# A fused attention and two mixture-of-experts kernel: one kind of matmul at a time, soft experts in pairs, a spread shared slot, a split last slot

## The chip, the cores and the metric

The kernel runs on one core of a Trainium2 chip, as one program. The metric is the device time of one execution in microseconds (us); less is better. Engines are named as the profile names them: PE is the matrix engine (PEld its weight loads), DVE, ACT and POOL are the vector, scalar and GpSimd engines, and SP is the engine whose queue issues most of the DMAs.

## The reference

Three layers follow one another on 1536 tokens of 512 features (2 batches of 768 tokens, 8 heads of 64). Everything is fp32.

```python
# 1 attention: key kept if among the first 8 (global) or 0..95 behind the query
scores = q @ k.T / 8 - slope[head] * dist        # -1e9 where not kept
a = softmax(scores, -1);  x = (a @ v) laid out as [1536, 512]
# 2 soft mixture: 8 experts, 4 slots each
logits = x @ phi                                 # [1536, 32]
d = softmax(logits, 0);   slot_in = d.T @ x      # over all tokens
h = relu(slot_in[e] @ w1[e]);  slot_out[e] = h @ w2[e]
x = softmax(logits, 1) @ slot_out
# 3 second mixture: 8 other experts, the best 2 for each token
noisy = x @ w_gate + log1p(exp(x @ w_noise)) * noise
out[token] += weight * (relu(x[token] @ w1[e]) @ w2[e])   # for its 2 experts
```

Each expert has w1 of 512x1024 and w2 of 1024x512, so each mixture reads 32 MB of weights.

## The kernel before, in words

**Attention** (functions `scores` to `stX`, loop over T = 0..12) takes 12 tiles of 128 queries, each in two halves, b0 = 2T and b1 = 2T + 1. For a half, PE multiplies 16 pairs of 64x64 weights by 167 keys into two PSUM banks (line 201); DVE adds the position bias and takes the row maximum in one custom instruction per bank half, four of them, into a tile `Tt` (205); ACT takes four exponentials with their sums (212); DVE inverts the sums (218, 219); POOL multiplies them in and lays the result out by key in `Pb` (227, 229); PE turns it, eight 128x128 transposes per half (237, tile `pt`); ACT copies that to `PT` (241). PE multiplies `PT` by the values `vt` (260), DVE copies the result, `xT` (267), and PE turns this back to tokens (`stX`, 277). POOL also copies the 8 global rows of the values from a small tile `gv` into each new `vt` (269, 271). After tiles 3, 7, 10 and 11 a segment (`seg`) updates the token softmax of layer 2 and adds into `U`. The order of the instructions on each engine is the order of this code.

**Weights.** The 32 MB of layer 2 come as 32 units of 1 MB, each half of a w1 or of a w2. Sixteen are issued during attention (line 372, in two DMAs of 0.5 MB, paced by `PACE`). Sixteen follow on the SP queue behind attention (682, two halves per unit): eight into a pool that lies where attention's tiles were, and eight into tiles that the first sixteen held (`AGAIN`). Then come the weights of layer 3 by `load_part` (735). SP runs its queue in order, and each issue waits for the eighth before it to have landed. Six DMAs of 0.5 MB that set the output to zero (`zero`, from a tile `zt`) are issued in tiles 5 to 10.

**Soft experts** (`ffn_a` 720, `ffn_t` 753, `ffn_b` 766): per expert PE does 32 matmuls with 32 weight columns for the first product, two 128x128 transposes of its activations, and 16 matmuls for the second product, which sums over all experts in one bank. The loop does a of expert e, t of e - 1, b of e - 2.

**Second mixture.** Weights become fp16 pairs (high and low part). Each expert has three slots of 128 tokens (24 in all, `NOWN`), each with 8 first products (1205), and three times 8 second products (1293), whose sum ACT scales into `ys` (1305) and POOL adds to the output with an indirect DMA (1311). A further "shared" slot (`Shared`) takes the tokens left over, 32 rows for each of four experts side by side: 8 steps `mm` (1176) of 12 small matmuls, a scaling, a joining matmul and one indirect add (1192). The table `SHARE` says after which part of which slot each of its steps stands: "0", "a", "m" and "p" are points inside a slot. The last slot's sum is scaled half on DVE (1302), then half on ACT (1303).

Adds of different experts may meet the same output row, so such an add waits for the one before to land; the three adds of one expert don't wait for one another.

Of the kernel before, what the change touches and what calls it, by code (L numbers as in the profile page):

```python
# [23 lines left out]
AGAIN = [0, 1, 4, 5, 8, 9, 12, 13]  # L24
PACE = lambda i: 1 + 4 * i // 3
KLOADS = {1: 3, 4: 6, 6: 9}
VLOADS = {1: 2, 4: 4, 6: 6, 8: 8, 10: 10}
ZEROS = [5, 6, 7, 8, 9, 10]
# [13 lines left out]
         (21, "0", "mm", 6), (21, "0", "mm", 7), (21, "0", "end"), (21, "a", "join"), (21, "m", "add", NOWN)]  # L42
# [6 lines left out]
NXS = 5  # L49
# [13 lines left out]
def emit(tc, d, near=True, stop=None):  # L63
    nc = tc.nc
    es = ExitStack()
    with es:
# [53 lines left out]
        phis = ac.tile([128, 4, 32], F32, name="phis")  # L120
        if near:
            ac.tile([128, 128], F32, name="Lsb")
            ac.tile([128, 128], F32, name="Et")
# [9 lines left out]
        pw = ps_o.tile([128, 512], F32, name="o")  # L133
# [57 lines left out]
        def scores(i, nm):  # L191
            Tt = wk.tile([128, 4, 167], F32, name="Tt", bufs=2)
            st = [ps_s.tile([128, 2, 167], F32, name="s") for _ in range(2)]
            m = i // 2 % 6
            for n in (2 * i, 2 * i + 1):
                T, p = divmod(n, 4)
                for t in range(2):
                    a = KS * m + 64 * t
                    for h in range(2):
                        g, r = slice(64 * h, 64 * h + 64), 64 * (h ^ t)  # L200
                        nc.tensor.matmul(st[t][r:r + 64, n % 2, :], qd[T % NQ][g, p, 64 * t:64 * t + 64], kx[g, p, a:a + 167],  # L201
                                         start=True, stop=True, tile_position=(64 * h, r))
            for k in range(4):
                j, t = divmod(k, 2)
                nc.vector.tensor_tensor_reduce(Tt[:, k], st[t][:, j], bias[:, int(m == 0), 2 * (i % 2) + j, t], -0.125, 1e30, ALU.add,  # L205
                                               ALU.min, nm[:, k:k + 1])
            S[i] = Tt
# [7 lines left out]
        def norm(i, st):  # L215
            Pu = S[i]
            r = sm.tile([128, 4], F32, name="r", bufs=3)
            nc.vector.tensor_scalar(r, st, 1e-9, None, ALU.add)
            nc.vector.reciprocal(r, r)  # L219
            Pn = Pb[i % NP]  # L220
# [52 lines left out]
        def stX(T):  # L273
            j = T % 4
            pxx = (ps_o if T < NT - 1 else ps_t).tile([128, 4, 128], F32, name="o" if T < NT - 1 else "pt")
# [22 lines left out]
        def seg(t0, w, psl):  # L298
# [10 lines left out]
            Lsb = ac.tile([128, 128], F32, name="Lsb", bufs=1)  # L309
            Et = ac.tile([128, 128], F32, name="Et", bufs=1)  # L310
# [7 lines left out]
            if near:  # L318
                nc.vector.tensor_copy(Lsb[P], psl[P])
                yield  # L320
                pe = (ps_o if late else ps_l).tile([128, 2, 128], F32, name="o" if late else "psl")
# [13 lines left out]
            else:  # L335
                pe = ps_o.tile([128, 2, 128], F32, name="o")
# [6 lines left out]
            pu = (ps_s if near and late else ps_o).tile([128, 512], F32, name="s" if near and late else "o")  # L343
# [13 lines left out]
        zt = lo.tile([128, 512], F32, name="zt")  # L357
        nc.gpsimd.memset(zt, 0.0)

        def zero(a, b):  # L360
            nc.sync.dma_start(out=out[a:b].rearrange("(p t) c -> p t c", p=128),
                              in_=zt.unsqueeze(1).to_broadcast([128, (b - a) // 128, 512]))

        def all_units():
            for k in range(NWA + NW):
                todo.extend(load_unit(k, wst if k < NW else wa, f"w{k}", 2))
            todo.reverse()
# [15 lines left out]
        def attention_near():  # L383
# [17 lines left out]
            segs, held = {}, {}  # L401

            def head(T):
                more_w(PACE(2 * T))
                st, nm = [sm.tile([128, 4], F32, name=k, bufs=3) for k in ("st", "nm")]
                scores(2 * T, nm)
                exps(2 * T, st, nm, (0, 1))
                return st, nm

            st0, nm = head(0)  # L410
            for T in range(NT + 1):
                new, b0, b1 = T < NT, 2 * T, 2 * T + 1
                if T in KLOADS:
                    load_k(KLOADS[T], 3)
                if T + 3 < NT:
                    load_q(T + 3)
                if T in VLOADS:
                    load_v(VLOADS[T])
                if T in ZEROS:
                    zero(256 * ZEROS.index(T), 256 * ZEROS.index(T) + 256)  # L420
                old = segs.pop(T - 3, None)
                if T - 4 in held:
                    list(held.pop(T - 4))
                if T < 2:
                    tables(1 - T, 2, 4)
                outs = [turn(n, True) for n in (2 * b0 - 4, 2 * b0 - 3)] if T else []
                for k, o in enumerate(outs):
                    o()
                    if new:
                        exps(b0, st0, nm, (2 + k,))  # L430
                if not new:
                    stX(T - 2)
                    segs[T - 2] = seg(*SEGS[T - 2], logits(*SEGS[T - 2]))
                if new and not outs:
                    exps(b0, st0, nm, (2, 3))
                if new:
                    more_w(PACE(b1))
                    st, nm = [sm.tile([128, 4], F32, name=k, bufs=3) for k in ("st", "nm")]
                    scores(b1, nm)
                    norm(b0, st0)  # L440
                    exps(b1, st, nm, (0,))
                outs = [turn(n, True) for n in (2 * b1 - 4, 2 * b1 - 3)] if T else []
                for k, o in enumerate(outs):
                    o()
                    if new:
                        exps(b1, st, nm, (1 + k,))
                if new:
                    exps(b1, st, nm, (3,) if outs else (1, 2, 3))
                if T == 0:
                    tables(0, 0, 2)  # L450
                fill(FILL.get(T, 0))
                if old:
                    next(old)
                if new and 0 <= T - 2:
                    stX(T - 2)
                if old:
                    next(old)
                if new and T - 2 in SEGS:
                    segs[T - 2] = seg(*SEGS[T - 2], logits(*SEGS[T - 2]))
                if T - 2 in SEGS:  # L460
                    next(segs[T - 2])
                if T + 1 < NT:
                    st0, nm = head(T + 1)
                if new:
                    norm(b1, st)
                if T - 2 in SEGS:
                    next(segs[T - 2])
                if T:
                    for n in range(2 * b0 - 4, 2 * b0):
                        values(n)  # L470
                if old:
                    next(old)
                    held[T - 3] = old
                if T:
                    valued(T - 1)
                if T == 1:
                    nc.gpsimd.memset(rn[0], 1e30)
                    nc.gpsimd.memset(rs, 0.0)
                    nc.gpsimd.memset(U, 0.0)
            more_w(2 * (NWA + NW))  # L480
            old = segs[T - 2]
# [10 lines left out]
        def attention_any():  # L492
# [4 lines left out]
            zero(0, NTOK)  # L497
# [81 lines left out]
        Lsb = ac.tile([128, 128], F32, name="Lsb", bufs=1)  # L579
        Et = ac.tile([128, 128], F32, name="Et", bufs=1)  # L580
# [25 lines left out]
        psi = ps_o.tile([128, 4, 32], F32, name="o")  # L606
# [134 lines left out]
        def ffn_a(e):  # L741
# [3 lines left out]
            hs = mw.tile([128, 256], F32, name="hs")  # L745
# [3 lines left out]
        def ffn_t(e):  # L749
            hs = hTs[e]  # L750
            pt = pm_([128, 2, 128])
            for i in range(2):
                nc.tensor.transpose(pt[:, i], hs[:, 128 * i:128 * i + 128], ident)

            hT = mw.tile([128, 2, 4, 32], F32, name="hT", bufs=3)
            nc.gpsimd.memset(hT, 0.0)
            es_ = slice(4 * e, 4 * e + 4)
            nc.vector.tensor_copy(hT[:, :, :, es_], pt.rearrange("p a (g s) -> p a g s", g=4)[:, :, :, es_])
            hTs[e] = hT
# [9 lines left out]
        with tc.manual_schedule(engines=hands):  # L769
            for e in range(NE + 2):  # L770
                if e < NE:
                    ffn_a(e)
                if 0 <= e - 1 < NE:
# [987 lines left out]
```

## Time and profile before

| what | value |
|---|---|
| median of 3 runs | 324.84 us (323.02 to 325.19) |
| the execution that was profiled, its own time | 324.2 us |
| its span, first to last instruction | 322.4 us |
| PE busy | 300.5 us, 93% |
| ACT, DVE, POOL busy | 206.9, 197.6, 129.5 us |
| data moved | 89.25 MB, mean 277 GB/s |
| PE clock granted | 0.98 over the span, below full in one early slice (16 to 24 us) and after the last matmul |

The profile is of one execution. Its stages, read from which lines run when: attention up to about 92 us, the joining of layer 2's slots up to 99, soft experts from 99 to 131, routing of the second mixture up to about 165 (slots begin inside it), slots up to 314, and the last add's landing up to 322. The time outside the span is 324.2 - 322.4 = 1.8 us.

### The profile page before, as it was taken

The numbers are of one execution on the slowest core, as the hardware profiler recorded it, in microseconds if no ns is written. First come the engines' busy times: TensorE is split into PE (matmuls) and PEld (weight loads), VectorE is DVE, ScalarE is ACT, GpSimd is POOL, SyncE is SP. The second block draws the span as 40 slices with busy tenths as digits, with TensorE's granted clock in tenths as the row PEclk, the third lists the DMA queues.
The fourth block names the chain that finished last, engine by engine and source line by source line (L and its number), as shares of the span: only waits on it lengthen the run. The fifth ranks groups of instructions, "written<-read, shape, count | busy, mean of one in ns | idle before, by whom it ended". The sixth has DMA issues, their size and how long they took to land. (4 is left out here: it accounts for less than half of the span.)

```text
span 322.4 us, 7769 instructions
## 1 busy us (share of the span) xinstructions
PE 300.5 (93%) x2860; PEld 169.7 (53%) x2860; DVE 197.6 (61%) x724; ACT 206.9 (64%) x490; POOL 129.5 (40%) x165
## 2 busy tenths in 40 slices
PE   8599999899999999998988999999999999999990
PEld 3367877678766443444544445554454445544540
DVE  1746667667555000299768796969687586996210
ACT  2759887888633111299759786869788686685400
POOL 3355555464601100213443857642617335261131
PEclk9959999999999999999999999999999999999996
DMA  8999999997999999999899779497999943404352
GB/s 252 362 401 347 331 370 403 405 405 250 406 409 410 408 408 403 411 407 409 325 344 344 167 176 245 64 349 241 222 334 337 339 73 43 68 1 53 48 67 39
DMA packets 30651, 89.25 MB, mean 277 GB/s; under 512 B 2816, under 2 KB 6656, under 8 KB 30608
## 3 DMA queue, kind: packets, MB, share of 16 engines
q1 hardware_dynamic: 25920, 80.70, 65.7%
q0 software_dynamic: 4400, 7.48, 15.7%
q10 hardware_dynamic: 288, 0.52, 0.6%
q8 instruction: 24, 0.39, 0.5%
q14 instruction: 19, 0.16, 0.1%
HBM read 78.55 MB, written 10.14 MB: 275 GB/s over the span
## 5 line engine op out<-in xcount | busy, mean ns | idle before, releaser
L1293 PE MATMUL y<-w2hl,hh 128*128 128x512 f16 x552 | 125.1, 379 | 0.8 <-ACT w2hl L1307 0.8
L1293 PEld LDWEIGHTS <-hh 128*128 128x128 f16 x552 | 52.2, 98 | 61.7 <-issue 4.8
L227 POOL TENSOR_TENSOR Pb<-Tt,r 128x668 f32<-128x668 f32 x24 | 32.1, 1336 | 43.9 <-DVE r L219 32.2
L212 ACT ACTIVATE Tt<-Tt,nm 128x167 f32<-128x167 f32 x96 | 40.8, 427 | 10.3 <-DVE nm L205 10.2
L1214 DVE SCALAR_TENSOR_TENSOR hh<-h,hh 128x512 f16<-128x512 f32 x46 | 29.6, 684 | 20.7 <-ACT hh L1206 20.7
L1311 POOL DMA_INDIRECT out_y<-ys,sidx x15 | 27.9, 1857 | 30.4 <-ACT ys L1305 16.1
L205 DVE CUSTOM_DVE_ANT_0 Tt<-s,bias 128x167 f32<-128x167 f32 x96 | 26.1, 328 | 22.6 <-POOL Pb L229 9.3
L890 DVE SCALAR_TENSOR_TENSOR w2hl<-w,pm,w2hl 128x1024 f16<-128x1024 f32 x28 | 35.2, 1280 | 3.3 <-ACT w2hl L887 2.4
L1329 POOL DMA_INDIRECT cT<-ctab,gidx x25 | 27.6, 1105 | 13.7 <-DVE pm L844 6.7
L1206 ACT ACTIVATE hh<-h 128x512 f16<-128x512 f32 x46 | 25.1, 598 | 12.0 <-PE h L1205 10.1
L241 ACT ACTIVATE PT<-pt 128x512 f32<-128x512 f32 (+1 forms) x48 | 26.2, 551 | 8.4 <-PE pt L237 8.2
L887 ACT ACTIVATE w2hl<-w,pm 128x1024 f16<-128x1024 f32 x28 | 31.2, 1147 | 0.2 <-DVE pm L843 0.2
L237 PE MATMUL pt<-c,Pb 128*128 128x128 f32 x176 | 25.5, 287 | 5.1 <-POOL Pb L227 2.6
L858 ACT ACTIVATE w2hl<-w 128x1024 f16<-128x1024 f32 x28 | 29.5, 1059 | 0.0
L237 PEld LDWEIGHTS pt<-c,Pb 128*128 128x128 f32 x176 | 19.3, 144 | 12.4 <-POOL Pb L229 4.4
L1311 POOL DMA_INDIRECT out_y<-c,sidx x7 | 11.2, 1595 | 33.1 <-ACT w2hl L887 12.6
L260 PE MATMUL px<-PT,vt 128*64 128x128 f32 x352 | 22.7, 283 | 0.0
L201 PE MATMUL s<-kx,qd 64*64 64x167 f32 x384 | 21.0, 321 | 1.6 <-DVE nm L205 1.5
L260 PEld LDWEIGHTS px<-PT,vt 128*64 128x64 f32 x352 | 19.7, 141 | 2.9 <-issue 2.5
L212 ACT ACTIVATION_READ_ACCUMULATOR Tt<-Tt,nm 128x1 f32 x96 | 18.3, 191 | 0.0
L201 PEld LDWEIGHTS s<-kx,qd 64*64 64x64 f32 x384 | 13.2, 135 | 7.4 <-issue 6.4
L1205 PEld LDWEIGHTS <-Gst 128*128 128x128 f16 x192 | 12.7, 98 | 7.1 <-issue 1.8
(315 smaller groups left out, 445.6 us busy)
## 6 DMA issues: line engine op xcount, KB each, us to landing
w<-in_w2b SPq DMA_DIRECT2D x14, 1024.0 KB, 12.7
x<-in_w1b SPq DMA_DIRECT2D x12, 1024.0 KB, 10.2
w<-in_w1a SPq DMA_DIRECT2D x16, 512.0 KB, 8.8
w<-in_w2a SPq DMA_DIRECT2D x16, 512.0 KB, 10.2
w<-in_w1a SPq DMA_DIRECT2D x8, 1024.0 KB, 14.6
w<-in_w2a SPq DMA_DIRECT2D x8, 1024.0 KB, 11.7
vt<-in_va SPq DMA_DIRECT2D x6, 512.0 KB, 5.8
out_y<-zt SPq DMA_DIRECT2D x6, 512.0 KB, 7.1
```

The source lines that it names most:

```text
L201: nc.tensor.matmul(st[t][r:r + 64, n % 2, :], qd[T % NQ][g, p, 64 * t:64 * t + 64], kx[g, p, a:a + 167], start=True, stop=True, tile_posit ...
L212: nc.scalar.activation(Tt[:, k], Tt[:, k], AF.Exp, bias=nm[:, k:k + 1], scale=-1.0, accum_out=st[:, k:k + 1])
L227: nc.gpsimd.tensor_tensor(wide(Pn, 33, 264 + 64, 528, 167), Pu.rearrange("p (a t) c -> p a t c", t=2), rb(167), ALU.mult)
L237: nc.tensor.transpose(pt[:, ch, t], Pn[:, 2 * (n % 2) + t, 136 * ch:136 * ch + 128], ident)
L260: nc.tensor.matmul(px[64 * h:64 * h + 64, p, :], vv[:, c:c + 64], cols_, start=(ch == 0 or m == 0), stop=(ch == 1))
L858: nc.scalar.activation(w2hl[:, self.r, 1, 2 * q:2 * q + 2], self.quarter(q), AF.Abs, accum_out=self.wm[:, q:q + 1])
L887: nc.scalar.activation(w2hl[:, self.r, 0, 2 * q:2 * q + 2], self.quarter(q), AF.Copy, scale=self.sw)
L890: nc.vector.scalar_tensor_tensor(w2hl[:, self.r, 1, 2 * q:2 * q + 2], self.quarter(q), self.sw, w2hl[:, self.r, 0, 2 * q:2 * q + 2], ALU.m ...
L1214: nc.vector.scalar_tensor_tensor(hh[:, 1, 4 * q:4 * q + 4], phs[q], 0.0, hh[:, 0, 4 * q:4 * q + 4], ALU.max, ALU.subtract)
L1293: nc.tensor.matmul(py, hh[:, hx, f], w2hl[:, e, wx, f], start=(n == 0), stop=(n == 23))
L1311: o = nc.gpsimd.indirect_dma_start(out=out, out_offset=bass.IndirectOffsetOnAxis(ap=sidx[:, j:j + 1], axis=0), in_=ys, in_offset=None, com ...
L1329: nc.gpsimd.indirect_dma_start(out=cgf[:, place(n)], out_offset=None, in_=ctab, in_offset=bass.IndirectOffsetOnAxis(ap=gidx[:, n:n + 1], a ...
```

## The change

- Attention does one kind of PE work per tile: all 32 score matmuls of a tile in a row into four banks, then the 32 value matmuls of tile T - 2 (T - 1 before), then the turns of tile T - 1 with `stX` of T - 3 between them. `Tt` has three buffers instead of two. The normalisation of b1 stands in the next tile's iteration.
- Pool `ps_s` grows to four banks, `ps_x` shrinks to one, `ps_o` is gone.
- The output's zeros become one DMA behind the first slots' start (after `go`), before the loads of expert 3.
- The units come in another order (`UNITS`): w1 of experts 0 to 5 and w2 of 0 and 1 during attention, then w1 of 6, 7 and w2 of 2, 3, then w2 of 4 to 7 into tiles of the w1 of experts 2 to 5.
- The soft experts run in pairs: two a, one t with four transposes for both, two b.
- The shared slot's `mm` steps stand in slots 20, 21 and 22 (20 and 21 before), its add between those of slots 21 and 22 (between 20 and 21 before).
- The last slot's second product is done for 256 columns and then for the other 256, in two banks, with 48 matmuls of half the width; ACT scales both halves.

```diff
-AGAIN = [0, 1, 4, 5, 8, 9, 12, 13]
+UNITS = [4 * e + i for e in range(6) for i in (0, 1)] + [2, 3, 6, 7]
+UNITS += [24, 25, 28, 29, 10, 11, 14, 15, 18, 19, 22, 23, 26, 27, 30, 31]
+AGAIN = [4, 5, 6, 7, 8, 9, 10, 11]
-VLOADS = {1: 2, 4: 4, 6: 6, 8: 8, 10: 10}
-ZEROS = [5, 6, 7, 8, 9, 10]
+VLOADS = {0: 2, 4: 4, 6: 6, 8: 8, 10: 10}
...
-         (20, "a", "mm", 1), (20, "a", "copy", 3), (20, "a", "copy", 4), (20, "m", "mm", 2), (20, "m", "mm", 3),
-         (20, "m", "copy", 5), (20, "p", "copy", 6), (20, "b", "mm", 4), (20, "b", "mm", 5), (21, "0", "copy", 7),
-         (21, "0", "mm", 6), (21, "0", "mm", 7), (21, "0", "end"), (21, "a", "join"), (21, "m", "add", NOWN)]
+         (20, "m", "copy", 3), (20, "p", "copy", 4), (21, "0", "mm", 2), (21, "0", "mm", 3), (21, "0", "copy", 5),
+         (21, "a", "copy", 6), (21, "m", "mm", 4), (21, "m", "mm", 5), (21, "m", "copy", 7), (22, "0", "mm", 6), (22, "0", "mm", 7),
+         (22, "0", "end"), (22, "m", "join"), (22, "p", "add", NOWN)]
...
-        ps_s = pool("ps_s", 2, s_ps, space=PSUM)
+        ps_s = pool("ps_s", 4, s_ps, space=PSUM)
-        ps_x = pool("ps_x", 2, s_ps, space=PSUM)
+        ps_x = pool("ps_x", 1, s_ps, space=PSUM)
-        ps_o = pool("ps_o", 1, s_ps, space=PSUM)
-            wk.tile([128, 4, 167], F32, name="Tt", bufs=2)
+            wk.tile([128, 4, 167], F32, name="Tt", bufs=3)
...
             for T in range(NT + 1):
                 new, b0, b1 = T < NT, 2 * T, 2 * T + 1
+                last = sums.pop(T - 1, None)
+                if new:
+                    bank = scores(T)
+                    maxima(b0, bank, nm0, (0, 1))
+                if last:
+                    r1 = inverse(last)
+                    norm(b0 - 1, r1)
+                if new:
+                    maxima(b0, bank, nm0, (2, 3))
+                    exps(b0, st0, nm0)
+                    maxima(b1, bank, nm1, range(4))
+                    exps(b1, st1, nm1, (0,))
...
+                if T >= 2:
+                    for n in range(4 * T - 8, 4 * T - 4):
+                        values(n)
+                    valued(T - 2)
+                    if T in VLOADS:
+                        load_v(VLOADS[T])
+                outs = [turn(4 * T - 4 + p, True) for p in (0, 1)] if T else []
+                for o in outs:
+                    o()
+                if new:
+                    norm(b0, r0)
+                    exps(b1, st1, nm1, (1,))
+                if T >= 3:
+                    stX(T - 3)
+                if T:
+                    turn(4 * T - 2)
...
+                if T:
+                    turn(4 * T - 1)
+                if new:
+                    exps(b1, st1, nm1, (2, 3))
...
-            for o, src in load_unit(k, wb if i < NWB else wst if t < NW else wa, f"w{t}"):
+            for o, src in load_unit(UNITS[k], wb if i < NWB else wst if t < NW else wa, f"w{t}"):
...
+            ffn(ffn_a, 0)
+            halves()
+            ffn(ffn_a, 1)
+            ffn_t(0)
+            ffn(ffn_a, 2)
+            ffn_t(1)
+            ffn(ffn_b, 0)
+            make_ct()
+            ffn(ffn_a, 3)
+            ffn_t(2)
+            ffn(ffn_b, 1)
+            ffn_t(3)
+            ffn(ffn_b, 2)
+            ffn(ffn_b, 3)
...
+            if j == NOWN - 1:
+                for c in (slice(0, 256), slice(256, 512)):
+                    py = py if c.start == 0 else ps_y.tile([128, 512], F32, name="y")
+                    for i, (hx, wx) in enumerate(((0, 0), (0, 1), (1, 0))):
+                        for f in range(8):
+                            nc.tensor.matmul(py[:, c], hh[:, hx, f], w2hl[:, e, wx, f, c], start=(i == 0 and f == 0),
+                                             stop=(i == 2 and f == 7))
...
+                    nc.scalar.activation(ys[:, c], py[:, c], AF.Copy, scale=gs)
...
         nc.sync.value_load(go, min_val=1, max_val=1)
+        zero(0, NTOK)
         for i in range(2):
             fetch(3, i)
```

PE, one tile in the middle of attention, before (`s` scores, `px` values, `pt` turns, `o` the turn back to tokens):

```order
L201 MATMUL s<-kx,qd_106 64x167 x8
L260 MATMUL px<-PT,vt 64x128 x16
L237 MATMUL pt<-c_71,Pb_111 128x128 x8
L201 MATMUL s<-kx,qd_106 64x167 x8
L237 MATMUL pt<-c_71,Pb_112 128x128 x8
L277 MATMUL o<-c_71,xT 128x128 x4
```

and the same tile now:

```order
L199 MATMUL s<-kx,qd_103 64x167 x16
L266 MATMUL px<-PT,vt 64x128 x16
L243 MATMUL pt<-c_71,Pb_108 128x128 x8
L283 MATMUL s<-c_71,xT 128x128 x4
L243 MATMUL pt<-c_71,Pb_109 128x128 x8
```

Two runs of scores have become one, and the turn back to tokens stands between the two runs of turns.

SP, the last weight loads of attention and the first of the second half, before, with the engines whose semaphores each waits for:

```order
L372 DMA w_179<-in_w2a 128x1024 [waits DMAHW1_49]
L372 DMA w_179<-in_w2a 128x1024 [waits DMAHW2_49]
L682 DMA w_1712<-in_w1a 128x2x1024 [waits DMAHW3_49,PE_49]
L682 DMA w_1714<-in_w1a 128x2x1024 [waits DMAHW4_49,DVE_49]
L682 DMA w_1716<-in_w2a 128x2x1024 [waits DMAHW5_49,DVE_49,Activation_49]
```

and now:

```order
L371 DMA w_174<-in_w2a 128x1024 [waits DMAHW3_49]
L371 DMA w_174<-in_w2a 128x1024 [waits DMAHW4_49]
L675 DMA w_1700<-in_w1a 128x2x1024 [waits DMAHW5_49,Pool_49]
L675 DMA w_1702<-in_w1a 128x2x1024 [waits DMAHW6_49,DVE_49,PE_49]
L675 DMA w_1704<-in_w1a 128x2x1024 [waits DMAHW7_49]
```

The first load of the second half waited for PE (the last half-tile's scores); now it waits for POOL, for the last copy out of `gv`, whose place in SBUF it takes.

POOL, the last four adds to the output before:

```order
L1192 DMA out_y<-x_3943,sidx 1920x512 [waits DMASW5_49,DMASW4_49,DMASW6_49,DMASW3_49,Activation_49]
L1311 DMA out_y<-c_4237,sidx 1920x512 [waits DMASW6_49,Activation_49]
...
L1311 DMA out_y<-ys,sidx 1920x512 [waits DMASW0_49,Activation_49]
...
L1311 DMA out_y<-ys,sidx 1920x512 [waits Activation_49]
```

and now:

```order
L1328 DMA out_y<-c_4190,sidx 1920x512 [waits DMASW5_49,DMASW4_49,DMASW6_49,DMASW3_49,Activation_49]
L1333 MEMSET go 1x1 [waits Pool_49]
L1198 DMA out_y<-x_3943,sidx 1920x512 [waits DMASW6_49,Activation_49]
L1328 DMA out_y<-ys,sidx 1920x512 [waits DMASW7_49,DMASW0_49,Activation_49]
L1333 MEMSET go 1x1 [waits Pool_49]
L1328 DMA out_y<-ys,sidx 1920x512 [waits Activation_49]
```

The shared slot's add (line 1192 before, 1198 now) stands one add later, and the add of slot 22 now waits for its landing.

## Rows read from the trace of the kernel before

**Rows 1.** The page's rate of all transfers, in 40 slices of 8.06 us.

```profile
GB/s 252 362 401 347 331 370 403 405 405 250 406 409 410 408 408 403 411 407 409 325 344 344 167 176 245 64 349 241 222 334 337 339 73 43 68 1 53 48 67 39
```

**Rows 2.** Timeline of PE's weight loads, one tile (start, duration, idle before, releaser).

```profile
31.92 0.49 PEld L201 LDWEIGHTS s<-kx,qd 64*64 64x64 f32 x16 [0.17 <-issue]
32.65 1.73 PEld L260 LDWEIGHTS px<-PT,vt 128*64 128x64 f32 x32 [0.24 <-issue]
34.55 0.85 PEld L237 LDWEIGHTS pt<-c,Pb 128*128 128x128 f32 x8 [0.17 <-issue]
...
36.65 0.86 PEld L237 LDWEIGHTS pt<-c,Pb 128*128 128x128 f32 x8 [0.59 <-POOL Pb L229]
37.48 0.47 PEld L277 LDWEIGHTS o<-c,xT 128*128 128x128 f32 x4
```

**Rows 3.** Timeline of DVE, the longer of its two waits in that tile.

```profile
36.63 0.33 DVE L205 CUSTOM_DVE_ANT_0 Tt<-s,bias 128x167 f32<-128x167 f32 x1 [1.13 <-POOL Pb L229]
```

**Rows 4.** Timeline of ACT in that tile, one instruction of each kind.

```profile
32.21 0.58 ACT L241 ACTIVATE PT<-pt 128x512 f32<-128x512 f32 x1
...
33.10 0.42 ACT L212 ACTIVATE Tt<-Tt,nm 128x167 f32<-128x167 f32 x1
```

**Rows 5.** Timeline of POOL: the normalisation of b0 in tiles 3 and 11, then b1 of tile 11.

```profile
32.01 1.30 POOL L227 TENSOR_TENSOR Pb<-Tt,r 128x668 f32<-128x668 f32 x1 [1.05 <-ACT PT L241]
...
84.71 1.30 POOL L227 TENSOR_TENSOR Pb<-Tt,r 128x668 f32<-128x668 f32 x1 [1.97 <-ACT PT L241]
...
87.00 1.30 POOL L227 TENSOR_TENSOR Pb<-Tt,r 128x668 f32<-128x668 f32 x1 [0.79 <-DVE r L219]
...
88.44 0.60 POOL L271 COPY vt<-gv 8x512 f32<-8x512 f32 x1
```

**Rows 6.** Timeline of the SP queue, first load of the second half.

```profile
83.09 0.91 SPq L682 DMA_DIRECT2D w<-in_w1a  x2
```

**Rows 7.** Tile `w`, the DMA issued at 105.2 us (fourteenth load of that half).

```profile
L682 SPq DMA_DIRECT2D w<-in_w1a x1: 1067/1067/1067, 105.2 to 105.2; - x1
...
DMA to landing us min/median/max: 17.8/17.8/17.8
```

**Rows 8.** Tile `w`, the 0.5 MB DMA issued at 34.9 us: its landing.

```profile
DMA to landing us min/median/max: 4.4/4.4/4.4
```

**Rows 9.** Timeline of PE's weight loads, one soft expert, and the stage's last load.

```profile
121.53 0.20 PEld L753 LDWEIGHTS m<-c,hs 128*128 128x128 f32 x2 [0.41 <-issue]
121.89 0.16 PEld L766 LDWEIGHTS y<-w,hT 128*32 128x32 f32 x8 [0.17 <-issue]
...
125.47 0.20 PEld L753 LDWEIGHTS m<-c,hs 128*128 128x128 f32 x2 [0.41 <-issue]
...
130.67 0.13 PEld L766 LDWEIGHTS y<-w,hT 128*32 128x32 f32 x4 [0.30 <-issue]
```

**Rows 10.** Tile `w2hl`, first half of expert 2's w1, issued at 137.7: its landing.

```profile
DMA to landing us min/median/max: 14.4/14.4/14.4
```

**Rows 11.** Timeline of PE's weight loads, the first products with w1 of experts 2 and 3.

```profile
154.40 1.45 PEld L720 LDWEIGHTS pg<-w2hl,soT 128*32 128x32 f32 x32
...
188.35 1.45 PEld L720 LDWEIGHTS pg<-x,soT 128*32 128x32 f32 x32
```

**Rows 12.** Timeline of ACT, a slot beside that routing.

```profile
157.57 0.60 ACT L1206 ACTIVATE hh<-h 128x512 f16<-128x512 f32 x1 [1.50 <-PE h L1205]
```

**Rows 13.** Timeline of POOL, the first add and three of the last.

```profile
180.14 1.63 POOL L1311 DMA_INDIRECT out_y<-w2hl,sidx  x1 [0.30 <-issue]
...
300.61 1.57 POOL L1192 DMA_INDIRECT out_y<-x,sidx  x1 [4.23 <-ACT x L1189]
...
306.32 1.56 POOL L1311 DMA_INDIRECT out_y<-c,sidx  x1 [4.14 <-ACT hh L1206]
...
315.39 1.57 POOL L1311 DMA_INDIRECT out_y<-ys,sidx  x1 [4.00 <-ACTq L1554]
```

**Rows 14.** Timeline of ACT, its half of the last slot's scaling.

```profile
314.51 0.47 ACT L1303 ACTIVATE ys<-y,gsc 128x256 f32<-128x256 f32 x1 [5.01 <-DVE ys L1302]
```

More of the change, by code (lines that the diff above doesn't have):

```diff
@@ L219, in norm @@
             nc.vector.reciprocal(r, r)
+            return r
+        def norm(i, r):
+            Pu = S.pop(i)
             Pn = Pb[i % NP]
@@ L274, in stX @@
             j = T % 4
[L275 removed]
+            pxx = (ps_s if T < NT - 1 else ps_t).tile([128, 4, 128], F32, name="s" if T < NT - 1 else "pt")
             for p in range(4):
@@ L320, in seg @@
                 yield
-                pe = (ps_o if late else ps_l).tile([128, 2, 128], F32, name="o" if late else "psl")
+                pe = (ps_s if late else ps_l).tile([128, 2, 128], F32, name="s" if late else "psl")
                 nc.tensor.transpose(pe[:, 0, P], Et[P], ident[P, P])
@@ L342, in seg @@
                 nc.vector.tensor_copy(Ek[:, P], pe[:, 0, P])
-            pu = (ps_s if near and late else ps_o).tile([128, 512], F32, name="s" if near and late else "o")
+            pu = (ps_l if near and not late else ps_s).tile([128, 512], F32, name="psl" if near and not late else "s")
             for j in range(w):
@@ L355, in emit @@
         todo = []
[L357 to L362, printed above, removed]
         def all_units():
             for k in range(NWA + NW):
-                todo.extend(load_unit(k, wst if k < NW else wa, f"w{k}", 2))
+                todo.extend(load_unit(UNITS[k], wst if k < NW else wa, f"w{k}", 2))
             todo.reverse()
@@ L400, in attention_near @@
             tables(1, 1, 2)
[L401 to L410, printed above, removed]
+            segs, sums = {}, {}
             for T in range(NT + 1):
                 new, b0, b1 = T < NT, 2 * T, 2 * T + 1
+                more_w(PACE(b0))
                 if T in KLOADS:
@@ L431, in attention_near @@
[L431 to L435, printed above, removed]
-                if new:
[L437 to L446, printed above, removed]
-                if new:
-                    exps(b1, st, nm, (3,) if outs else (1, 2, 3))
+                last = sums.pop(T - 1, None)
+                if new:
+                    (st0, nm0), (st1, nm1) = [[sm.tile([128, 4], F32, name=k, bufs=3) for k in ("st", "nm")] for _ in range(2)]
+                    bank = scores(T)
+                    maxima(b0, bank, nm0, (0, 1))
@@ new lines, in attention_near @@
+                if last:
[4 more added lines that the diff above has]
+                    exps(b0, st0, nm0)
+                    if T < 2:
+                        tables(1 - T, 2, 4)
+                    maxima(b1, bank, nm1, range(4))
+                    exps(b1, st1, nm1, (0,))
+                old = segs.get(T - 4)
+                if old:
+                    list(old)
+                now = T - 3 in SEGS
@@ L449, in attention_near @@
+                if now:
+                    next(segs[T - 3])
+                    next(segs[T - 3])
                 if T == 0:
                     tables(0, 0, 2)
[L451 to L475, printed above, removed]
@@ L479, in attention_near @@
                     nc.gpsimd.memset(U, 0.0)
+                fill(FILL.get(T, 0))
             more_w(2 * (NWA + NW))
-            old = segs[T - 2]
+            stX(NT - 2)
+            old = segs[NT - 2] = seg(*SEGS[NT - 2], logits(*SEGS[NT - 2]))
+            next(old)
+            next(old)
+            for n in range(4 * NT - 4, 4 * NT):
+                values(n)
+            valued(NT - 1)
             fill(1, ps_t.tile([128, 512], F32, name="pt"))
@@ L1290, in slot_y @@
             n = 0
-            for hx, wx in ((0, 0), (0, 1), (1, 0)) if j > 3 else ((0, 0), (1, 0), (0, 1)):
+            if j == NOWN - 1:
+                ys = wk3.tile([128, 512], F32, name="ys", bufs=2)
+                for c in (slice(0, 256), slice(256, 512)):
[4 more added lines that the diff above has]
+                                             stop=(i == 2 and f == 7))
+                        if i == 1 or c.start == 0 and i == 2:
+                            yield
+                    nc.scalar.activation(ys[:, c], py[:, c], AF.Copy, scale=gs)
+            for hx, wx in () if j == NOWN - 1 else ((0, 0), (0, 1), (1, 0)) if j > 3 else ((0, 0), (1, 0), (0, 1)):
                 for f in range(8):
```

124 lines of the change are left out of this document (59 added, 65 removed), and 2 rows, old and new, of the table SHARE.

## The prediction

> **What bounds the kernel now.** I read the busy shares first: PE is at work for 93% of the span, so what counts is where PE's own work can shrink and whether something else then sets the pace. Next the rate of transfers by slice. From the eleventh slice (80.6 us) to the nineteenth (153 us) it stands at 403 to 411 GB/s without a dent [rows 1]. I take this plateau for the most that the transfers reach here, so from the soft experts to the routing of the second mixture there are two bounds side by side, PE and the stream of weights. To see how near they are I read landings: the fourteenth load of the second half was issued at 105.2 and landed 17.8 later, at 123.0 [rows 7]. At 405 GB/s a unit of 1.05 MB takes 2.59 us; 14 of them back from 123.0 gives 86.7. So the stream behaves as if it had started at 86.7, 3.6 after its first issue at 83.09 [rows 6], and its sixteenth unit lands at 86.7 + 16 x 2.59 = 128.2, where PE's soft experts end at 131.1 (a group of four loads begins at 130.67 and PE's gap is 0.30, rows 9). The first half of expert 2's w1 lands at 137.7 + 14.4 = 152.1 [rows 10], its second half one transfer later at 154.7, and PE wants the first half at 154.40 and the second 0.7 later, at 155.1 [rows 11]. The stream's slack is 0.4 us there. Before that, in attention, I read one tile on all engines: PE loads weights nearly without a break, and DVE waits 1.13 us for POOL to free one of two `Tt` [rows 3].
>
> **Attention.** The loads of a tile cost 0.49 + 1.73 + 0.85 + 0.49 + 0.86 + 0.47 = 4.89 us and the gaps 1.3 (0.17, 0.24, 0.17, 0.17, 0.59 behind POOL and a small rest), 6.19 in all, from 31.92 to the next scores at 38.11 [rows 2]. With one run per kind, three changes of kind remain between differently shaped loads, 0.24 + 0.17 + 0.17 = 0.58, so PE needs 5.47. ACT has eight exponentials of 0.42 and four copies of 0.58, which overlap by 0.1 (the rows follow one another at 0.48): 8 x 0.42 + 4 x 0.48 = 5.28 [rows 4]. POOL's two norms, at 1.6 with their small part, and a copy take under 4. With the third `Tt` nothing of DVE's wait remains in a cycle, so I take 5.5 per tile. From the norm of tile 3 to that of tile 11 it is now 84.71 - 32.01 = 52.7 [rows 5]; of this 3.2 is more than 8 x 6.19, the segments' share. I keep 2.7 of it, as the third buffer covers some, so 8 x 5.5 + 2.7 = 46.7, 6.0 less. For tiles 0 to 2, where tables and loads still matter, I take 1.7 of 3 x 0.7, so attention ends 7.7 earlier. The bounds: 9.5 if ACT's 5.28 holds, 5 if half of the gap stays.
>
> The transfers must follow. Queries, keys, values and 16 units are 9.4 + 16.8 = 26.2 MB, 2.2 per tile, which at 5.5 us is 400 GB/s; the zeros, 0.52 MB in each of six tiles, are gone from there. Slices of attention show 403 and 405 [rows 1], so it just fits. The Trainium skill, "DMA: Bandwidth & Descriptors", section "Specifications", gives an HBM limit of about 358 GB/s for a core; by it a tile's 2.2 MB would take 6.15 us (an estimate) and attention would gain nothing, the slower rival below. The measured 403 to 411 are above that figure, so I go by them.
>
> **What the second half's stream gains.** This is the step that decides. Its first load used to wait for the last scores. Now its place in SBUF covers `gv`, and it waits for POOL's last copy out of `gv`, behind the last norm. SP issues in order, so all sixteen units and the second mixture's weights are queued behind that wait. The last norm begins at 87.00 and the copy ends at 88.44 + 0.60 = 89.04 [rows 5]; 7.7 earlier is 81.3. So 7.7 us of attention buy only 83.1 - 81.3 = 1.8 at the first issue. The queue is then idle, and what an issue costs with little ahead of it is seen at 34.9: 0.5 MB, 1.3 of transfer, landed after 4.4 [rows 8], so at most 3.1 besides the transfer; from below I take 2.1, a third less, since something was ahead there too. The stream's start falls to 83.4 to 84.4 instead of 86.7, 2.3 to 3.3 earlier; I take 2.7. Between the end of attention's loads and this issue the transfers stand idle for some 8 us.
>
> **Soft experts in pairs.** One expert takes PE 3.94 us (121.53 to 125.47), and of each two experts one t and its gaps (0.41 + 0.17) go, 0.6 per pair, 2.4 in all [rows 9]. PE alone would end at 131.1 - 7.7 - 2.4 = 121.0. But the last unit lands at 128.2 - 2.7 = 125.5, and the last pair's b comes some 0.7 behind it. So the stage ends near 126.2, 4.9 earlier; the pairs' own gain is hidden by the stream, and so is the rest of attention's gain. The new order of the units puts the w2 of experts 4 to 7 last, which the last two pairs need only at the end: free.
>
> **Routing.** The stream is still the bound at expert 2's w1: 2.7 and the slack of 0.4 make 3.1 at 155. Behind it ACT waits 1.50 for PE's h [rows 12], and such waits of about 1 us can take up some of PE's earlier lead; I add 0.4, between 0 and 1. That makes 3.5.
>
> **Zeros.** 3.1 MB at 405 GB/s are 7.7 us of transfers, now ahead of expert 3's weights on SP near 160, in slices at 344 GB/s and then at 167 and 176 [rows 1]: 1.0 MB fits beside the first two, the rest into the next 9 us, to about 186. Expert 3's w1 is wanted at 188.35 [rows 11], and the first add at 180.14 [rows 13] waits for the zeros alone, which stand ahead of the weights and land near 170. I cost this at nothing; with the cover gone it is 7.7 on expert 3's first use.
>
> **Slots and tail.** The same matmuls, PE-bound. Spreading the shared steps can win back up to 0.9 of PE's waits for copied weights. In the last slot, DVE's and ACT's half stood in series; two banks would save ACT's 0.47 [rows 14]. 48 half-wide matmuls for 24 cost between 0 and 0.4 more. But the adds bind as well: 21's stood 5.7 us behind the shared one [rows 13], whose landing it had to await. Now the shared add follows 21's and slot 22's waits for it; counted back from PE's end (join behind 16 of slot 22's 24 products, 6.9 before; add 5.7 before) slot 22's add comes when PE ends, and the last 1.9 after, which is where it stands now (315.39, PE's end 313.5). So the two banks win nothing, and the tail is +0.3 (-1 to +1).
>
> **The sum.** 3.5 + 0.3 = 3.8. Against the profiled execution's 324.2 that is 320.4; the median of the runs stands 0.6 above that execution, so 321.0. A measurement of this kernel tells about 1%, 3.2 us, from no change.
>
> **The rivals.** (1) Attention gains only 5 to 6, because a wait on POOL or a PSUM bank stays in each tile. Each us lost there is a us lost at `gv`: the stream starts 0.1 to 1.0 earlier, 322.5 to 324.5. For it: ACT's and PE's sums are within 0.2 of each other, so neither covers the other's delays. Chance 0.20. (2) Slower: the period stays near 6.2, by transfers at 400 GB/s that come late or a chain of scores, maxima, norms and turns that closes on itself. Then attention ends only some 2.2 earlier, the first load goes at 86.8, the stream starts at 89.4, 2.7 later than now; less 0.4 of slack and 0.3 at the tail, 326.2, or 326.9 on the median. It decides from an attention gain below 4.9 (89.04 + 2.6 - 86.7). Chance 0.13. (3) The stream does not bind: the first load is held by less than I think, or runs ahead of PE. Then 7.7, the 2.4 and the tail's 0.3 all show: 10.4, 314.4. Against it stand the plateau and the slack of 0.4. Chance 0.10. (4) The change's tail costs its full 1 us and more, with the rest as forecast, 322.3; inside the forecast's range.
>
> **How the numbers follow.** The forecast has 0.57, with a range of its own of 318.8 to 322.8 (stream's start 2.3 to 3.3, routing 0 to 1, tail -1 to +1). Of it about two thirds lie below 321.6, the 1% mark: 0.39. With rival 3, faster has 0.49. Rival 1 and the rest of the forecast lie within 1%, and about a half of rival 2: 0.18 + 0.20 + 0.07 = 0.45. Slower than 328.1 has 0.06: rival 2 with a tail that loses too, or a maxima-norm chain over 6.2. The range 316.5 to 326.5 holds the forecast, rival 1, a third of rivals 2 and 3 each: about 0.84.
>
> **What would show it.** In the profile after: score runs 5.5 apart; the SP queue's first second-half load right behind POOL's copy out of `gv` near 81 us; a hole in the transfers before it; the soft experts waiting for weights at their end, near 126; expert 2's routing product near 151; zeros between 157 and 175 with no wait at expert 3; the last two adds 1.9 apart. I am wrong if the first load goes well before the copy's end, if PE waits for no weights in the soft experts, or if the last add stands further than 2 us from PE's end.

## The result, and the profile after

The changed kernel takes 328.52 us (median of 4 runs, 327.6 to 329.48) against 324.97 before; the ratio is 1.0134, 95% interval 1.0099 to 1.0169. It is slower by 3.6 us where 3.8 faster was forecast. The execution that was profiled took 329.48 us, 1 above its median, with a span of 327.3.

I look at the transfers first, by slice as in [rows 1] (a slice is 8.18 us here):

```profile
GB/s 256 370 398 397 399 363 357 412 125 237 75 410 410 407 409 404 410 407 409 368 334 375 408 262 244 66 273 326 272 327 253 350 80 40 70 16 51 33 38 67
```

Three slices from 65 to 90 us stand at 125, 237 and 75 where before there were 405, 250 and 406. The first of them is a hold inside attention: nothing is issued from 59.5 to 71.8, because a load of values (`vt`) stands there in SP's order and waits 12.3 us for PE's products on the tile that it overwrites. PE does not feel that one: it waits for no transfer in these tiles. The SP queue tells when attention's weights end (start and duration of the issues, merged; `vt` values, L371 attention's weights, L675 second half; compare [rows 6]):

```profile
71.80 0.33 SPq L152 DMA_DIRECT2D vt<-in_va  x1
72.17 1.38 SPq L371 DMA_DIRECT2D w<-in_w2a  x3
86.75 2.16 SPq L675 DMA_DIRECT2D w<-in_w1a  x4
```

Attention's last weights are issued at 73.5, and then nothing for 13 us; the transfers stand at 6 GB/s from 80 to 88. The first load goes at 86.75, 3.7 later than before, right behind POOL's copy out of `gv`, as the norms' timeline shows (b0 of tiles 3 and 11, b1 of tile 11, the copy; compare [rows 5]):

```profile
30.30 1.30 POOL L233 TENSOR_TENSOR Pb<-Tt,r 128x668 f32<-128x668 f32 x1 [0.26 <-DVE xT L273]
...
81.30 1.30 POOL L233 TENSOR_TENSOR Pb<-Tt,r 128x668 f32<-128x668 f32 x1 [0.58 <-PE pt L243]
...
84.69 1.30 POOL L233 TENSOR_TENSOR Pb<-Tt,r 128x668 f32<-128x668 f32 x1 [1.88 <-DVE r L221]
...
86.13 0.60 POOL L277 COPY vt<-gv 8x512 f32<-8x512 f32 x1
```

The copy ends at 86.73 instead of 89.04: attention gained 2.3 us and not 7.7. One tile on PE (compare [rows 2]) shows that the run order itself worked:

```profile
37.14 1.06 PEld L199 LDWEIGHTS s<-kx,qd 64*64 64x64 f32 x32 [0.17 <-DVE xs L289]
38.43 1.73 PEld L266 LDWEIGHTS px<-PT,vt 128*64 128x64 f32 x32 [0.24 <-issue]
40.33 0.85 PEld L243 LDWEIGHTS pt<-c,Pb 128*128 128x128 f32 x8 [0.17 <-issue]
41.15 0.47 PEld L283 LDWEIGHTS s<-c,xT 128*128 128x128 f32 x4
41.80 0.86 PEld L243 LDWEIGHTS pt<-c,Pb 128*128 128x128 f32 x8 [0.17 <-issue]
```

The next scores begin at 37.14 + 5.68. What took the gain back are tiles with a segment. PE stops twice for the copy (`Lsb`, DVE) that the segment's transposes read:

```profile
50.57 0.14 PEld L328 LDWEIGHTS psl<-c,Et 128*128 128x128 f32 x1 [1.22 <-DVE Lsb L325]
...
75.42 0.14 PEld L328 LDWEIGHTS psl<-c,Et 128*128 128x128 f32 x1 [1.23 <-DVE Lsb L325]
```

Before, the same two transposes followed the turns without a gap (at 50.57, behind loads of 49.69 + 0.91, and at 76.70, behind 75.83 + 0.91).

Then the late stream binds. PE waits for the last unit of the soft experts and for the second half of expert 2's w1, whose products stood at 155.1 before ([rows 11], plus half of the run):

```profile
131.63 0.16 PEld L759 LDWEIGHTS y<-w,hT 128*32 128x32 f32 x8 [2.38 <-DMA w<-in_w2a]
...
158.02 0.59 PEld L713 LDWEIGHTS pg<-w2hl,soT 128*32 128x32 f32 x16 [1.00 <-DMA w2hl<-in_w1b]
```

That is 2.9 later at 158. From there to the slots nothing is won back (expert 3's first product goes 3.3 later, 191.61 for 188.35), and some 1.1 more is lost at one place: PE waits 1.24 for a small DVE result (`wx`, line 866) at 236.5, where before it did not. `wx` stands in DVE's order behind work on a slot's first products, which ACT takes (line 1212) at 233.14, although PE's row for them ends at 232.07; before, ACT took them as PE's row ended (228.69 for 228.82). What ACT waited for there, no row shows.

The chain of adds at the tail (compare [rows 13]) goes as it was worked out: slot 22's add waits for the shared add's landing, 5.45 after its issue, and the last add follows 1.86 later:

```profile
311.56 1.57 POOL L1198 DMA_INDIRECT out_y<-x,sidx  x1 [4.58 <-ACT x L1195]
317.01 1.56 POOL L1328 DMA_INDIRECT out_y<-ys,sidx  x1 [3.88 <-DMA out_y<-x,sidx]
...
318.87 1.57 POOL L1328 DMA_INDIRECT out_y<-ys,sidx  x1 [0.27 <-issue]
```

### The profile page after: what moved, and what is told of

Its sections match the earlier page's. It is cut to its first block, busy times and chain, and to the rows that moved or that the text cites. A ratio compares the mean times of both kernels' runs of the same rounds, so it can differ in the third digit from the quotient of the medians.

```text
span 327.3 us, 7818 instructions
## 1 busy us (share of the span) xinstructions
PE 297.6 (91%) x2884; PEld 172.0 (53%) x2884; DVE 197.5 (60%) x723; ACT 207.7 (63%) x491; POOL 125.9 (38%) x165
## 5 line engine op out<-in xcount | busy, mean ns | idle before, releaser
L1310 PE MATMUL y<-w2hl,hh 128*128 128x512 f16 x528 | 120.4, 379 | 0.5 <-ACT w2hl L1324 0.5
L1310 PEld LDWEIGHTS <-hh 128*128 128x128 f16 x528 | 49.7, 98 | 58.3 <-issue 4.1
L1328 POOL DMA_INDIRECT out_y<-ys,sidx x15 | 25.3, 1684 | 29.1 <-ACT ys L1322 14.2
L1346 POOL DMA_INDIRECT cT<-ctab,gidx x25 | 26.4, 1056 | 14.5 <-DVE w2hl L890 8.0
L247 ACT ACTIVATE PT<-pt 128x512 f32<-128x512 f32 (+1 forms) x48 | 24.7, 558 | 8.4 <-PE pt L243 8.3
L243 PE MATMUL pt<-c,Pb 128*128 128x128 f32 x176 | 24.7, 282 | 5.6 <-ACT PT L247 4.0
L199 PE MATMUL s<-kx,qd 64*64 64x167 f32 x384 | 18.1, 323 | 1.0 <-DVE nm L209 1.0
L1333 POOL MEMSET go<- 1x1 int32 x24 | 16.8, 700 | 0.0
## 6 DMA issues: line engine op xcount, KB each, us to landing
w<-in_w2a SPq DMA_DIRECT2D x12, 1024.0 KB, 11.5
```

The lines of the kernel that those rows point to most:

```text
L243: nc.tensor.transpose(pt[:, ch, t], Pn[:, 2 * (n % 2) + t, 136 * ch:136 * ch + 128], ident)
L1310: nc.tensor.matmul(py, hh[:, hx, f], w2hl[:, e, wx, f], start=(n == 0), stop=(n == 23))
L1328: o = nc.gpsimd.indirect_dma_start(out=out, out_offset=bass.IndirectOffsetOnAxis(ap=sidx[:, j:j + 1], axis=0), in_=ys, in_offset=None, com ...
L1346: nc.gpsimd.indirect_dma_start(out=cgf[:, place(n)], out_offset=None, in_=ctab, in_offset=bass.IndirectOffsetOnAxis(ap=gidx[:, n:n + 1], a ...
```

## The experiments

Theory A: the hold on `gv` is what costs. The load that starts the second half waits for an event of attention's end, SP's order passes that wait on to all weights behind it, and the loss is the lateness of the stream. Theory B: PE's own work costs, and the hold is hidden behind it.

**e1_gv, the hold taken away.** The small tile moves to another pool; the order on every engine stays word for word.

```diff
-            gvt = ac.tile([8, 512], F32, name="gv")
+            gvt = lo.tile([8, 512], F32, name="gv")
```

> The changed kernel with one edit: the small tile gv lies in another pool, so the first load of the second half waits for the last scores and no longer for POOL's copy out of gv. The order of every engine stays. Theory A (the wait on gv opens a hole of 14.7 us in the transfers, from 72 to 86.7, and the stream is then late by 3.3 at expert 2's w1): the first load goes near 77 instead of 86.75, the soft experts end near 128.2 on PE alone instead of 131.8, and the time is some 3.6 lower, 324.9 us (323.5 to 326). Theory B (the loss lies in PE's own work, segments, pairs and a lower clock, and the hold is hidden): 328.5, the first load early but the end unchanged.

Measured: 324.95 us, ratio to before 1.001 (0.9976 to 1.0043). The whole loss is gone, as A said to 0.1 us. The SP queue and two windows of e1_gv (after the stretch: PE, PEld, DVE, ACT, POOL busy with their counts, granted clock, DMA share, GB/s):

```profile
77.95 3.06 SPq L675 DMA_DIRECT2D w<-in_w1a  x4
88.52 23.20 SPq L675 DMA_DIRECT2D w<-in_w2a  x12
```
```profile
100.00:102.00 2.00, 2.00 (x24) 1.08 (x20) 1.38 (x4) 0.87 (x2) 0.00 (x0) 0.50 0.45 180
102.00:104.00 2.00, 2.00 (x40) 1.14 (x36) 0.14 (x1) 0.37 (x2) 0.00 (x0) 0.96 0.04 14
```

The first load goes 8.8 earlier. The soft experts' last group of loads stands at 130.22, though, and not near 128.2 as expected: the next experiments find out why. And a second hold of the same kind comes to light: the transfers run dry from 101 to 105, because the ninth load goes into a tile that the third expert's product reads (SP waits 9.1 us for it). In the changed kernel the stream was so late that this never showed.

**e2_hold, the hold added to the kernel before.** `gv` moves the other way, to where the first load goes.

```diff
-            gvt = ac.tile([8, 512], F32, name="gv")
...
         qd = [ac.tile([128, 4, 128] if near else [128, 4, 2, 128], F32, name=f"qd{i}") for i in range(NQ)]
         if near:
+            gvt = ac.tile([8, 512], F32, name="gv")
```

> The kernel before with one edit: gv lies where the first load of the second half goes, so that this load waits for POOL's last copy out of gv (89.04) instead of the last scores (83.09). Theory A: the stream starts 5.7 later, 92.4 instead of 86.7, less 0.4 of slack, 5.3 slower: 330 us (328.5 to 331). Theory B (the hold is hidden): 325.

Measured: 331.21 us, ratio 1.0208 (1.0152 to 1.0264), so 6.3 slower; A gave 5.3, B nothing. It lies 0.2 above A's range: the first load goes 5.9 later than before (88.99 for 83.09), but expert 2's first product 6.2 (160.63 for 154.40). SP's issues, and the longer of PE's two waits for weights in the soft experts:

```profile
88.99 0.90 SPq L682 DMA_DIRECT2D w<-in_w1a  x2
```

```profile
125.97 0.59 PEld L720 LDWEIGHTS h<-w,siT 128*32 128x32 f32 x16 [3.14 <-DMA w<-in_w1a]
```

Two moves of a tile of 2 KB per partition, one off and one on, each with its cost: the hold is shown from both sides.

**e3_share, the shared slot's table of before in the changed kernel.** Only `SHARE` goes back.

> The changed kernel with the table of the shared slot's steps of before: its add stands again between those of slots 20 and 21. Tail theory: the adds of slots 22 and 23 stand 5 us apart again instead of 1.9, so the last add lands in 7.0 after its issue and not 8.4; 0.4 of waits for copied weights come back; 327.5 us (327 to 328). If the tail costs nothing: 328.5 to 329.

Measured: 328.06 us, ratio 1.0096 (1.0066 to 1.0126), 0.5 below the changed kernel, within the intervals of both. POOL's last adds in e3_share:

```profile
313.33 1.57 POOL L1328 DMA_INDIRECT out_y<-ys,sidx  x1 [2.12 <-ACT ys L1322]
...
318.48 1.57 POOL L1328 DMA_INDIRECT out_y<-ys,sidx  x1 [3.54 <-ACTq L1572]
```

The adds are 5.15 apart again, as expected, but the span still ends 8.4 after the last one (326.9 - 318.48). So the nearness of two adds is not why the end takes 8.4 us in some executions and 7.0 in others; that part of the expectation fell. What does go with it stands below, at the tail.

**e4_gv_tail, e1 with the old table and the old last slot.** Three undone parts, no new code.

> Both edits, gv in another pool and the table of before, and the last slot in one bank as before, scaled by DVE and ACT. If theory A and the tail theory add up: 323.7 us (322.5 to 325), against 324.9 for gv alone; by theory B with the tail theory 327.5.

Measured: 324.22 us, ratio 0.9979 (0.9952 to 1.0005). The tail's share is 0.7, inside the intervals: its direction is that of the expectation, its size can't be told from nothing.

**e5_again, the second hold moved.** On e4:

```diff
-AGAIN = [4, 5, 6, 7, 8, 9, 10, 11]
+AGAIN = [0, 1, 2, 3, 4, 5, 6, 7]
```

> As e4 (gv in another pool, old table, old last slot), with one more edit: the last eight units go into the tiles of the w1 of experts 0 to 3 instead of 2 to 5, so the ninth load of the second half waits for the first expert's product and not the third's. In e1 the transfers stood at 14 to 180 GB/s from 100 to 105 for that wait, and PE then waited 0.4 and 0.8 for w1 of experts 1 and 2. Theory A with a second hold: both waits go, 1.1 lower, 323.1 us (322 to 324). If PE alone binds: 324.2.

Measured: 324.86 us, ratio 1.0015 (0.998 to 1.0049). A miss: not 1.1 lower. The hole from 101 to 105 closes (279 GB/s from 100 to 102, 395 behind it), but another opens later, and the second half of expert 2's w1 is used 1.5 later than in e4 (156.76 for 155.24). e6 shows why.

**e6_warm, PE kept at work while layer 2's slots are joined.** On top of e5:

```diff
-            fill(1, ps_t.tile([128, 512], F32, name="pt"))
+            fill(2, ps_t.tile([128, 512], F32, name="pt"))
             psl = logits(*SEGS[NT - 1])
...
-        warm(2)
+        warm(5)
```

> As e5, with four more fp16 matmuls on unused data in PE's waits while layer 2's slots are joined (one more ahead of the last logits, three more behind the last turn). In e1 the granted clock stood at half from 98.5 to 102, in the first two experts' products; in the kernel before it did not fall there. Clock theory: it stays full, half of 3.3 us comes back, 1.6 lower than e5, 321.5 us. If the clock falls anyway or the stream binds: e5's time or 0.5 above.

Measured: 324.46 us, ratio 0.9991 (0.996 to 1.0021). The clock did as expected, but of the 1.6 only 0.4 show in the medians, which can't be told from nothing. The first products of the soft experts in e5_again, then in e6_warm:

```profile
98.00:100.00 2.00, 1.99 (x24) 1.19 (x27) 1.72 (x6) 0.00 (x0) 0.82 (x3) 0.73 1.03 418
100.00:102.00 2.00, 2.00 (x24) 1.04 (x20) 1.25 (x4) 0.83 (x2) 0.00 (x0) 0.50 0.77 279
```

```profile
98.00:100.00 2.00, 1.99 (x35) 1.26 (x38) 1.72 (x6) 0.00 (x0) 0.82 (x3) 1.00 0.96 367
100.00:102.00 2.00, 2.00 (x44) 1.20 (x40) 1.31 (x4) 0.89 (x2) 0.00 (x0) 1.00 0.85 285
```

In e5 PE was busy 5.62 of the 6 us from 90 to 96 and then fell to the level of 1.2 GHz for some 3 us; in e6 it was busy 5.89 and did not fall. The last group of the soft experts' loads begins at 128.60 instead of 130.34, 1.7 earlier. But at the second half of expert 2's w1 this only makes good what e5's table had lost (e4, e5, e6 in this order):

```profile
155.24 0.59 PEld L713 LDWEIGHTS pg<-w2hl,soT 128*32 128x32 f32 x16 [0.74 <-DMA w2hl<-in_w1b]
156.76 0.59 PEld L713 LDWEIGHTS pg<-w2hl,soT 128*32 128x32 f32 x16 [1.02 <-DMA w2hl<-in_w1b]
155.05 0.59 PEld L713 LDWEIGHTS pg<-w2hl,soT 128*32 128x32 f32 x16 [0.95 <-DMA w2hl<-in_w1b]
```

The windows and SP's queue of e6_warm tell why:

```profile
110.00:120.00 10.00, 10.00 (x122) 4.20 (x124) 0.58 (x4) 1.70 (x4) 0.92 (x3) 1.00 1.03 410
120.00:125.00 5.00, 5.00 (x48) 1.62 (x44) 0.29 (x2) 0.00 (x0) 0.62 (x2) 1.00 0.48 185
125.00:130.00 5.00, 4.64 (x44) 1.17 (x36) 0.00 (x0) 0.30 (x1) 0.00 (x0) 1.00 0.64 238
```

```profile
125.41 1.23 SPq L728 DMA_DIRECT2D w<-in_w1b  x2
```

The second mixture's first w1 goes into tiles 2 and 3. With e5's table these hold the w2 of expert 5, which is read near the end, so its load goes at 125.41 (127.15 in e5) instead of 114.49 (e4). I had traded one hold for another.

**e7_seg, the segments' transposes behind the next tile's scores.** On e5:

```diff
                 if old:
-                    list(old)
+                    next(old)
+                    next(old)
...
                     load_v(VLOADS[T])
+                if old:
+                    list(old)
...
-                if now:
-                    next(segs[T - 3])
-                    next(segs[T - 3])
```

> As e5, with the segments' transposes moved from the end of tiles 6 and 10 to the next tile, behind its scores, and the product that adds to U moved behind the values. In the changed kernel PE waited 1.22 and 1.23 for DVE at those transposes. Theory that the segments took attention's gain: about 1.2 lower at each, 2.4 in all on attention's end, 1.5 to 2.4 below e5, 321 us. If attention's end is covered by the stream: e5's time.

Measured: 325.24 us, ratio 1.0022 (0.9985 to 1.006). The time shows nothing of it. The rows are much like e6's: the soft experts begin at 96.81 instead of 98.42, 1.6 earlier, and their last group of loads stands at 128.72, but expert 2's second half is used at 155.31, no earlier than in e4, for the same hold (the second mixture's first load goes at 125.53).

**e8_single, one expert at a time, on e5.** The soft experts' loop of before.

> As e5, with the soft experts' order of before (a of e, t of e - 1, b of e - 2, one expert at a time). With the stream no longer held, PE binds this stage, so the pairs' 0.6 for two experts shows: 2.4 above e5, 325.5 us. If the stream binds there still: e5's time.

Measured: 326.28 us, ratio 1.0053 (1.0025 to 1.0082), 1.4 above e5, where 2.4 was expected. Where the stream doesn't hold PE, the pairs are worth 1.2 (last group of loads at 131.52 instead of 130.34), half of the 2.4 that I had counted.

**e9_all, the holds behind attention taken away.** e4 with e6's and e7's edits, and a table that reuses tiles 0 and 1 (read first) but leaves 2 and 3 free:

```diff
-AGAIN = [4, 5, 6, 7, 8, 9, 10, 11]
+AGAIN = [0, 1, 4, 5, 6, 7, 8, 9]
```

> e4's edits (gv in another pool, old table, old last slot) with e6's four matmuls and e7's move of the segments, and the last eight units in the tiles of the w1 of expert 0 and of experts 2 to 4 (0, 1, 4 to 9). In e5 to e7 tiles 2 and 3 held a w2 that is used late, and the second mixture's first w1, which goes there, was issued at 125.4 instead of 114.5: a hole at 185 to 240 GB/s from 120 to 130. Theory (each hold of the queue by a tile that comes free late is paid in full; PE otherwise): no hole between 100 and 130, soft experts' end at 127.0 instead of 130.3 (1.7 for the clock, 1.6 for the segments), no wait for w1 of experts 1 and 2, 3.3 to 4.4 below e4's 324.2: 320.5 us (319.5 to 322). If routing is bound by ACT and DVE: 323.

Measured: 321.12 us (9 runs, 319.67 to 323.19), ratio 0.9901 (0.9862 to 0.994): faster than both kernels, and within 0.6 of what was worked out. The stream of e9_all has no hole left between 100 and 130, and SP issues the second mixture's w1 at 110.53:

```profile
100.00:110.00 10.00, 10.00 (x168) 5.68 (x164) 2.90 (x10) 3.32 (x8) 0.00 (x0) 1.00 0.99 386
110.00:120.00 10.00, 10.00 (x127) 4.16 (x119) 0.29 (x2) 1.44 (x3) 1.23 (x4) 1.00 1.03 412
120.00:130.00 10.00, 9.49 (x86) 3.18 (x78) 0.71 (x3) 0.39 (x1) 0.31 (x1) 1.00 1.03 405
```

```profile
75.62 3.66 SPq L675 DMA_DIRECT2D w<-in_w1a  x4
...
110.53 3.57 SPq L728 DMA_DIRECT2D w<-in_w1b  x2
```

Expert 2's first product stands at 151.51 (154.40 before), with no wait for a weight. The edits of e6 and e7, each worth nothing measurable on e5, stand here with a table that holds nothing back; which of the three carries how much of the gain over e4 (0.78% by the two ratios, 2.5 us) was not separated.

**e10_single, one expert at a time, with the hold in place.** The changed kernel with the loop of before.

> The changed kernel with the soft experts one at a time, as before; the hold on gv stays. The prediction's step that the stream hides the pairs: the stage waits for its last unit at 131.6 and PE alone would be there at 128.2 with pairs and 129.4 without (e8 showed 1.2), so no change, 328.5 us (327.8 to 329.2). If PE's work counts there: 329.7.

Measured: 328.41 us, ratio 1.0101 (1.0037 to 1.0165), the changed kernel's time. The last group of loads stands at 131.62, as with pairs (131.63). So under the hold the stream hides the pairs. It is these rows that show it: the time, of four runs, has an interval of about 2 us to either side, too wide to tell 1.2 from nothing.

## Why the prediction was wrong, point by point

**The step that failed is the size of attention's gain**, 7.7 us; 2.3 came. The start-up gave its 1.7 (norm of tile 3 at 30.30 for 32.01). From tile 3 to 11 I had 6.0 and got 1.7: 51.0 us (81.30 - 30.30) for 52.7. Of the missing 4.3 the period, 5.68 for 5.5, is 1.4: I had counted three gaps between runs of loads, and there are four of 0.17 to 0.24, one of them between the turn back and the second run of turns, whose shape is the same. The larger part is the segments: 51.0 - 8 x 5.68 = 5.6, where I kept 2.7 of a share that was 3.2 before. That share grew by 2.4, and PE's new waits of 1.22 and 1.23 for DVE's copy are just that. The last 1.1 is a term that I put at nothing: the last half-tile, which used to follow its partner by 2.3, follows by 3.4 (81.30 to 84.69). I carried a segment over as a sum of instructions and did not follow the chain PE, ACT, DVE, PE in the new order. That these waits were worth their time on PE, e7 shows: with the transposes moved, the soft experts begin 1.6 earlier.

**The hold was seen, and its price was too low.** The prediction's break-even, 4.9 us of attention, lay above the 2.3 that came, so the kernel lost as rival 2 has it. e1 and e2 show the hold as the cause. But I took 2.7, at most 3.1, from the first issue to the start of the stream, since the queue would be idle; it was about 3.5, as before. In the changed kernel the tenth load of the half, issued at 104.7, lands 11.5 later, at 116.2; ten units of 2.59 back gives 90.3, and the first issue was at 86.75. So by the prediction's own steps 2.3 of attention make expert 2's w1 2.2 later (2.6 less the slack of 0.4), and it was 2.9. What I failed to do was to doubt the 7.7 enough: between forecast and loss lay one row of the queue.

**Rival 2 came near with its number, by another way.** It wanted a period near 6.2, from late transfers or from a chain of scores, norms and turns. Neither was there: the period was 5.68, with waits of 0.17 behind DVE and none behind a DMA. That it, too, had attention gain some 2.2 is luck: segments and the last half-tile took what it gave to the period. Its 326.9 lies 1.6 below the measured 328.5; the price above and the wait for `wx` are of that size. The Trainium skill, "DMA: Bandwidth & Descriptors", section "Specifications", has about 358 GB/s as the limit of a core; this case's windows show 404 to 412 for tens of us (412 from 110 to 120 in e9_all), so the measurement decides here.

**Soft experts.** That the stage is bound by the stream, and that the pairs are hidden, came true (2.38 of wait at the last unit; e10). The pairs' worth was half of what I counted (e8). That PE's clock would fall at the start of this stage was not in the prediction at all (granted clock 0.66 from 97 to 102 in the changed kernel); without the hold it costs 1.7 of this stage (e5 against e6). Under the hold PE waits 2.38 for the last unit, more than that, so I take it to cost nothing there; no run shows it.

**Zeros.** Free, as costed: their DMA goes at 163.4, PE has no wait for weights at expert 3, and from expert 2's second half to expert 3's first product it is 33.6 us (158.02 to 191.61) where it was 33.25. No run puts the zeros back.

**Tail.** The chain of adds came as worked out (5.45 and 1.86 between them); undoing the table gave 0.5, undoing table and last slot 0.7, neither beyond its interval. The rows say more than the times. On PE the spread steps give back 0.7: from the product on `wx` at 236.54 to PE's end at 317.61 it is 81.07, and in e3_share, with the old table, 81.81 (235.76 to 317.57). Behind PE's end the changed kernel takes 9.7 us where it took 8.4 (322.4 - 313.96; the 313.5 that I gave for PE's end was misread, and the last add stood 1.4 behind it, not 1.9). This goes with the last slot and not with the table: the four profiled executions with the last slot in two banks (the changed kernel, e1, e3, e10) end 7.5 to 8.6 after the last add's issue, the eight with one bank 6.8 to 7.2. I had put the two banks at nothing. No run undoes the last slot alone, so this is a coincidence of rows and not a cause shown. Of the profiled execution's 4.9 us of longer span, 2.9 stand at 158, 3.3 at expert 3, 4.4 behind the wait for `wx`, 3.7 at PE's end, and the rest comes behind it.

**What stays open:** the wait of 0.8 to 1.3 us for `wx`, in eight profiled executions (the changed kernel, e2, e3, e5, e6, e8, e9 and e10) and absent before and in e1, e4 and e7; and why the end comes later after the last add where the last slot has two banks.

## What to carry to other kernels

When memory is reused, the address of a small tile is a wait: before a load that heads an in-order queue, look up which instruction last reads each byte under it, and give that place to something that dies early. A gain ahead of such a queue is worth only as much as moves the event that the queue waits for, so work out its break-even first and ask how sure the gain is. And when two edits show nothing alone, look for the hold behind them before dropping them.

## What was not expected of the hardware

PE's clock fell where PE had hardly paused. In e5 PE was busy 5.62 of the 6 us from 90 to 96, and the granted clock then fell from the level of 2.4 to that of 1.2 GHz for some 3 us (0.50 from 100 to 102). In e6, with four more matmuls on unused data (5.89 of 6), it did not fall. Nor did it in the kernel before, with 5.90 of 6 there, though PE idled more in the 4 us after (3.42 of 4 busy).
